# Layer weights by GpSimd's casting DMA, and q of every second pair turned by the DMA crossbar, in an attention-then-MLP kernel

## The chip, the cores and the metric

The kernel runs on one core of a Trainium2 chip. The metric is the device time of one execution in microseconds; lower is better. Times of one kernel are medians over its executions. A ratio is the mean time of one kernel's fast runs over the mean of the other's fast runs of the same rounds, so it is not quite the ratio of the medians quoted beside it. A result is called faster or slower only beyond 2%.

Names: PE is TensorE, PEld its weight loads, DVE VectorE, ACT ScalarE, POOL GpSimd, SP the sync engine, whose queue issues most DMAs. A transpose by the DMA crossbar is a DMA_TRANSPOSE in the trace, and a DMA's landing is its completion as the trace reports it. "L305" is a line of the kernel; the changed kernel's lines are shifted by up to 14 against those of the kernel before.

## The reference

```python
scores = q @ k.T / 8                      # 8 batches x 8 heads, 576 tokens, head size 64
thresh = max(scores, -1) - 0.02
scores = where(scores >= thresh, scores, -1e9)
attn   = softmax(scores)
x      = (attn @ v)                       # -> 4608 tokens x 512
h = x @ w_in;  g = h - tanh(h);  out = g @ w_out     # 512 -> 2048 -> 512, float32
```

## The kernel before

Two heads make a pair; there are 32 pairs (four to a batch), and each has nine tiles of 128 queries. Step s of the one big loop computes scores of tile s+7, makes shifted scores z of those of tile s+4, turns the z of tile s into softmax weights, and uses the weights of tile s-2 on v. From the second batch on, z is turned by a DMA through the crossbar (zT), and a share of the MLP of the batch before is put into every step. The kernel is emitted in a fixed order: each engine, and SP's queue, executes its instructions in that order.

q and k are split on GpSimd into two float16 halves (`hl`), turned on TensorE by nine transposes each, and copied out of PSUM by VectorE:

```python
def turn(p, t):
    hl = hls.pop((p, t))
    ps = ps_big.tile([P, W], FP16, name=f"ps_{t}", tag="big")
    for c in range(TPP):
        turn_chunk(ps[:, c * P : (c + 1) * P], c, hl[:, c, :, :].rearrange("p a d -> p (a d)"))
    m = qk_pool.tile([P, W], FP16, name=f"{t}T", tag=t)
    nc.vector.tensor_copy(out=m, in_=ps)
    mats[p, t] = m
    if t == "k":                          # kS: the halves swapped
        ...
            if p < HPAIR:
                nc.sync.dma_start(out=o, in_=i)
            else:
                nc.gpsimd.tensor_copy(out=o, in_=i)
```

The layer weights are loaded as float32 by SP into two buffers and cast by GpSimd; a load waits for the cast two before it:

```python
def w_cast():
    flat, wt, i, cols = loaded.pop(0)
    nc.gpsimd.tensor_copy(out=flat[:, i * cols : (i + 1) * cols], in_=wt)
def w_load(piece):
    ...
    wt = wt_pool.tile([P, cols], F32, name="wt", tag="wt")      # 2 buffers
    nc.sync.dma_start(out=wt, in_=s)
```

Preparation of a pair is planned by steps before its first score (LDK is 16), at the end of the step:

```python
PREP = ((LDK, load k), (LDK - 1, load q), (LDK - 2, load v), (8, split k), (7, split q),
        (5, turn k), (3, turn q), (4, split_v))
first = TPP * p - AHEAD                   # the step that holds the pair's first score
```

## Time and profile before

| | before |
|---|---|
| time, median of 4 | 557.35 us (556.17 to 559.22) |
| TensorE busy | 517.2 us of 555.2 us, 93% |
| TensorE busy from 250 to 300 us | 49.3 of 50 us |
| VectorE, ScalarE, GpSimd busy | 81%, 79%, 51% |
| DMA share from 250 to 300 us | 0.83 |

The table is read by stages. Until about 75 us attention of the first batch runs alone and TensorE has gaps; from 77 us the MLP is mixed in, and from about 140 us TensorE is nearly gapless; after 480 us only MLP is left. The lines are shown in the prediction.

### The profile page before, as it was taken

What the parts mean: (1) busy time and instruction counts of PE and PEld (TensorE: products, weight loads), DVE (VectorE), ACT (ScalarE), POOL (GpSimd) and SP (SyncE); (2) the same over time, 40 slices, a digit from 0 to 9 for tenths busy, and PEclk for the clock granted to TensorE, in tenths of its full rate; (3) what the DMA queues carried; (4) which work ended last, traced back from release to release, by engine and by line L of the source; (5) the groups of instructions that cost most, each with busy time, mean ns of one, the idle gap of its engine ahead of it and who ended that gap; (6) DMA issues with size and microseconds to landing.
All of it is one profiled execution on the core that took longest, in us unless ns stands there. A gap on an engine that the chain in (4) does not pass through costs nothing.

```text
span 555.2 us, 13146 instructions
## 1 busy us (share of the span) xinstructions
PE 517.2 (93%) x4806; PEld 296.8 (53%) x4806; DVE 450.5 (81%) x1210; ACT 439.5 (79%) x624; POOL 280.6 (51%) x378
## 2 busy tenths in 40 slices
PE   5787978889999999999999999999999999899997
PEld 2565645455555555555555555555555555444444
DVE  5877899998998999898988999888989998644440
ACT  4888879998988898889898898888988899733330
POOL 7466996666665565556556666656545650000000
PEclk9989999999999999999999999999999999999999
DMA  6776599887897798788888898889887775410103
GB/s 187 213 216 188 185 222 186 168 154 161 164 170 178 176 173 181 169 158 179 173 171 164 161 190 170 172 160 176 161 194 172 153 150 114 96 40 38 39 38 76
DMA packets 205280, 86.55 MB, mean 156 GB/s; under 512 B 172448, under 2 KB 197280, under 8 KB 205216
## 3 DMA queue, kind: packets, MB, share of 16 engines
q1 hardware_dynamic: 204624, 85.30, 71.1%
q8 instruction: 37, 0.61, 0.5%
q10 hardware_dynamic: 592, 0.43, 0.3%
q14 instruction: 27, 0.22, 0.1%
HBM read 37.75 MB, written 9.44 MB: 85 GB/s over the span
## 4 chain that ended last, share of the span: by engine, by line
PE 68%; DVE 14%; issue 6%; DMA 4%; POOL 4%; ACT 3%; SPq 1%; POOLq 0%; ACTq 0%; DVEq 0%
PE psY L483 20%; PE psH L457 16%; PE psS L292 15%; PE psO L402 5%; DVE sc L302 4%; DVE g L476 3%; PE psHt L457 2%; PE psS L282 2%; PE ps_q L217 2%; DMA zT<-z 2%; PE ps_k L217 2%; DVE nb L316 2%; DVE yo L493 2%; DVE qT L229 1%; PE psO L391 1%
## 5 line engine op out<-in xcount | busy, mean ns | idle before, releaser
L302 DVE TENSOR_SCALAR_CACHE_REDUCE sc<-psS 128x576 f32<-128x576 f32 x288 | 214.3, 751 | 17.2 <-PE psS L292 9.3
L336 ACT ACTIVATE z<-sc,nb 128x576 bf16<-128x576 f32 x256 | 192.4, 767 | 26.4 <-DVE nb L316 26.1
L373 ACT ACTIVATE pT<-zT 128x1152 f16<-128x1152 bf16 (+1 forms) x140 | 149.4, 1067 | 6.5 <-DMA zT<-z 4.8
L483 PE MATMUL psY<-w_out_sb,g 128*128 128x512 bf16 (+1 forms) x592 | 146.0, 374 | 0.0
L238 POOL COPY kS<-kT 64x1152 f16<-64x1152 f16 x56 | 63.9, 1141 | 142.3 <-DVE nb L316 141.0
L457 PE MATMUL psH<-xT,w_in_sb 128*128 128x512 bf16 x480 | 123.4, 379 | 2.3 <-DVE g L476 2.3
L292 PE MATMUL psS<-kT,qT 128*128 128x512 f16 (+1 forms) x512 | 106.2, 289 | 10.8 <-DVE nb L316 3.7
L292 PEld LDWEIGHTS <-qT 128*128 128x128 f16 x1024 | 77.1, 98 | 72.6 <-issue 17.7
L476 DVE SCALAR_TENSOR_TENSOR g<-th,psH 128x512 bf16<-128x512 f32 x128 | 87.2, 682 | 24.7 <-ACT th L470 24.7
L292 PE MATMUL psS<-kS,qT 128*128 128x512 f16 x496 | 102.3, 288 | 0.2 <-DMA kS<-kT 0.2
L470 ACT ACTIVATE th<-psH 128x512 f32<-128x512 f32 x128 | 74.8, 584 | 33.9 <-PE psH L457 33.3
L483 PEld LDWEIGHTS <-g 128*128 128x128 bf16 x592 | 50.9, 98 | 56.5 <-issue 3.1
L457 PEld LDWEIGHTS <-w_in_sb 128*128 128x128 bf16 x576 | 48.9, 98 | 59.1 <-issue 5.6
L402 PEld LDWEIGHTS <-pT 128*128 128x128 f16 x1280 | 55.9, 98 | 26.0 <-ACT pT L373 3.0
L402 PE MATMUL psO<-vb,pT 128*128 128x65 bf16 x1280 | 61.6, 194 | 0.6 <-ACT pT L373 0.6
L316 DVE TENSOR_SCALAR nb<-mx 128x2 f32<-128x2 f32 (+1 forms) x160 | 42.9, 268 | 0.8
L179 POOL TENSOR_TENSOR qhl<-xs,qhl 128x576 f16<-128x576 f32 x31 | 39.7, 1279 | 2.7
L179 POOL TENSOR_TENSOR khl<-xs,khl 128x576 f16<-128x576 f32 x31 | 39.6, 1279 | 2.6
L217 PE MATMUL ps_k<-ident_f,khl 128*128 128x128 f16 x288 | 22.2, 223 | 13.9 <-POOL khl L179 7.4
L229 DVE COPY qT<-ps_q 128x1152 f16<-128x1152 f16 x31 | 23.5, 757 | 11.0 <-PE ps_q L217 10.9
L365 ACT ACTIVATE pT<-psZ 128x640 f16<-128x640 bf16 (+1 forms) x36 | 23.6, 655 | 10.4 <-PE psZ L356 10.3
L493 DVE COPY yo<-psY 128x512 f32<-128x512 f32 (+1 forms) x31 | 21.1, 680 | 10.7 <-PE psY L483 6.7
(71 smaller groups left out, 522.2 us busy)
## 6 DMA issues: line engine op xcount, KB each, us to landing
vraw<-in_v_dram SPq DMA_DIRECT2D x32, 256.0 KB, 3.5
out_dram<-yo SPq DMA_DIRECT2D x32, 256.0 KB, 2.8
kraw<-in_k_dram SPq DMA_DIRECT2D x31, 256.0 KB, 3.2
qraw<-in_q_dram SPq DMA_DIRECT2D x31, 256.0 KB, 3.7
wt<-in_moe_w_in_dram SPq DMA_DIRECT2D x8, 512.0 KB, 4.8
wt<-in_moe_w_out_dram SPq DMA_DIRECT2D x8, 512.0 KB, 4.3
vraw<-in_v_dram SPq DMA_DIRECT2D x64, 32.0 KB, 3.0
zT<-z SPq DMA_TRANSPOSE x112, 3.4
```

The source lines that it names most:

```text
L179: nc.gpsimd.tensor_tensor(out=hl[:, :, 1, :], in0=x, in1=hl[:, :, 0, :], op=ALU.subtract)
L238: nc.gpsimd.tensor_copy(out=o, in_=i)
L292: nc.tensor.matmul(out=ps[:, dst], lhsT=lhs, rhs=kk[:, src], start=(n == 0), stop=(n == 1),)
L302: nc.vector.tensor_scalar(out=sc, in0=ps[:, lo : lo + S], scalar1=SC, scalar2=None, op0=ALU.mult, op1=ALU.max, accum_out=mx[:, c : c + 1],)
L316: nc.vector.tensor_scalar(out=nb[:, 0:n], in0=mx[:, 0:n], scalar1=-1.0, scalar2=tau, op0=ALU.mult, op1=ALU.add,)
L336: nc.scalar.activation(out=z, in_=sc, func=ACT.Prelu, bias=nb, scale=1.0, alpha=STEEP)
L373: nc.scalar.activation(out=pt[:, 0 : n * P], in_=zts.pop(i)[:, 0:n, :], func=ACT.Exp)
L402: nc.tensor.matmul(out=po[:, (j - 1 - 5 * hh) + ab, :], lhsT=pt[:, blk * P : (blk + 1) * P], rhs=vb[:, hh, c, :], start=(n == 0), stop=(n ...
L457: nc.tensor.matmul(out=ps, lhsT=w_in_sb[:, c, n * P : (n + 1) * P], rhs=xs[m][:, c, :] if m < B else xR[:, c, :, :], start=(c == 0), stop= ...
L470: nc.scalar.activation(out=th, in_=ps, func=ACT.Tanh)
L476: nc.vector.scalar_tensor_tensor(out=gs[m][:, n, :], in0=th, scalar=-1.0, in1=ps, op0=ALU.mult, op1=ALU.add,)
L483: nc.tensor.matmul(out=ps, lhsT=gs[m][:, n, ms * P : (ms + 1) * P], rhs=w_out_sb[:, n, cols], start=(n == 0), stop=(n == DF_C - 1),)
```

## The change

The intent: let GpSimd's queue load and cast the weights in one DMA, so that no cast and no wait for a buffer is left; and take nine transposes and a copy of every second q from TensorE and VectorE.

```diff
-    wt_pool = pool("wt", 2)
...
+    def q_by_dma(p):
+        return p >= 2 * HPAIR and p % 2 == 1
+
     def turn(p, t):
         hl = hls.pop((p, t))
+        if t == "q" and q_by_dma(p):
+            m = mats[p, t] = qk_pool.tile([P, W], FP16, name=f"{t}T", tag=t)
+            nc.sync.dma_start_transpose(
+                out=m.rearrange("p (c r) -> p c r", c=TPP),
+                in_=hl.rearrange("p c a d -> p (c a d)"),
+            )
+            return
...
         if j == 4:
+            qrem = REM
+            if q_by_dma(p):
+                qrem = (slice(512, 640, 2), slice(513, 640, 2))
-                            lhsT=qT[:, REM[hh]], rhs=kk[:, srcs[hh]],
+                            lhsT=qT[:, qrem[hh]], rhs=kk[:, srcs[hh]],
...
-            if s + AHEAD in w_when:
-                if loaded:
-                    w_cast()
-                piece = next(pieces, None)
-                if piece:
-                    w_load(piece)
+        if s + AHEAD in w_when:
+            dst, src = next(pieces)
+            nc.gpsimd.dma_start(out=dst, in_=src)
```

## The prediction

> **What bounds the kernel now.** I read the page first, then the busy time by stage, then the chain of waits for the first 140 us, and last the timelines of single engines around one pair boundary.
>
> ```profile
> PE 517.2 (93%) x4806; PEld 296.8 (53%) x4806; DVE 450.5 (81%) x1210; ACT 439.5 (79%) x624; POOL 280.6 (51%) x378
> ...
> DMA  6776599887897798788888898889887775410103
> ```
>
> ```profile
> 28.00:50.00 22.00, 19.77 (x271) 14.51 (x271) 18.36 (x57) 19.24 (x32) 13.71 (x19) 0.94 0.68 188
> 50.00:75.00 25.00, 18.89 (x238) 13.39 (x238) 19.56 (x54) 18.75 (x31) 22.69 (x28) 0.93 0.74 214
> ...
> 250.00:300.00 50.00, 49.29 (x469) 28.04 (x467) 45.47 (x124) 44.40 (x61) 31.35 (x43) 1.00 0.83 173
> ```
>
> The columns are window, length, busy us of PE, PEld, DVE, ACT, POOL, then clock, DMA share, GB/s. There are two regimes. From about 140 us PE is busy for 49.3 of 50 us and sets the pace; DVE and ACT stand at 91% and 89%. Before 75 us PE has gaps, and POOL is at 22.7 of 25. The POOL timeline says why:
>
> ```profile
> 22.90 1.04 POOL L584 CAST w_in_sb<-wt 128x1024 bf16<-128x1024 f32 x1 [6.16 <-DMA wt<-in_moe_w_in_dram]
> ...
> 36.48 1.04 POOL L584 CAST w_in_sb<-wt 128x1024 bf16<-128x1024 f32 x1 [3.87 <-DMA wt<-in_moe_w_in_dram]
> ...
> 51.12 1.04 POOL L584 CAST w_in_sb<-wt 128x1024 bf16<-128x1024 f32 x1 [4.92 <-DMA wt<-in_moe_w_in_dram]
> ```
>
> POOL stands still in front of a cast whose load has not landed. The splits of the next pair's k and q queue behind it, so TensorE turns k late, and ScalarE waits in turn (4.42 us at 57.57 us). The chain of waits from 15.7 to 54.9 us lies wholly on POOL. So the weights are on the path early, and TensorE is the path later.
>
> **What the skill says.** (1) The Trainium skill, "DMA: Bandwidth & Descriptors", section "SWDGE vs HWDGE vs iDMA": a cast in a DMA needs the GpSimd queue, a plain DMA transpose the SP or ACT queue. The change obeys both; the trace shows all 140 transposes on SP. (2) The same page, "Issuing engines are not separate DMA queues": all issuers share 16 DMA engines, and another issuer saves only issuing time. So the weights' 8 MB still pass through these engines; what goes is the buffer and the wait. No run here shows GpSimd's issuing cost yet. (3) The same page, "Anatomy of one DMA": a fixed cost near 2.0 us, mostly the receipt. The trace agrees: a full transpose lands about 1.97 us (median of two of the groups) after its 1.3 us issue ends, also when another went just ahead.
>
> **Part A, weights.** It removes 16 casts (16 x 1.04 = 16.6 us of POOL), POOL's 15.7 us wait for the loads, and 16 loads from the SP queue. It adds 16 issues on POOL, perhaps 1 us each (my guess), none with a wait. What it is worth is read from ScalarE: from its first pT (18.3 us) to the end of its last of the first batch (71.6 us) 53.3 us pass, of which it idles 9.1 us (2.01, 0.17, 0.45, 1.03, 0.22, 4.42, 0.25, 0.28, 0.23). Where it is unhindered, one tile takes 1.21 to 1.25 us (z and pT, e.g. five tiles from 33.36 to 39.39); 36 tiles need 44 to 45 us. That would gain 8 to 9 us. TensorE, at 90% and a clock of 0.94, and the later k loads will keep some; less weight traffic at 75 to 100 us, where DMA is at 0.99 and one zT takes 6.56 us, gives some. I book -7 us.
>
> **Part B, q of 12 pairs (9, 11, ... 31).** Removed per pair: nine transposes on TensorE and one DVE copy.
>
> ```profile
> L229 DVE COPY qT<-ps_q 128x1152 f16<-128x1152 f16 x31 | 23.5, 757 | 11.0 <-PE ps_q L217 10.9
> ...
> zT<-z SPq DMA_TRANSPOSE x112, 3.4
> ```
>
> The chain gives ps_q x9 as 0.52 us of TensorE, so 12 x 0.52 = 6.2 us of the bound; the copies are 12 x 0.76 = 9.1 us of DVE, which is beside the path. Added: 12 transposes of the same shape as the full zT (128 x 1152, two bytes), 12 x 1.32 = 16 us of SP issuing and 12 x 1152 = 13,800 packets, 7% of 205,280. If nothing waited, B would be -6 us.
>
> But q must be there when the next pair's first score is due, and the issue keeps its place in the program: end of the step three before it, in order on SP, behind that step's zT. Here is the boundary to pair 13, first SP, then PE:
>
> ```profile
> 181.97 1.25 SPq L344 DMA_TRANSPOSE zT<-z  x1
> ...
> 187.74 0.57 SPq L139 DMA_DIRECT2D vraw<-in_v_dram  x1
> 188.37 0.66 SPq L145 DMA_DIRECT2D vraw<-in_v_dram  x1
> 189.08 0.62 SPq L146 DMA_DIRECT2D vraw<-in_v_dram  x1
> 189.80 1.32 SPq L344 DMA_TRANSPOSE zT<-z  x1
> 191.22 1.24 SPq L344 DMA_TRANSPOSE zT<-zm  x1
> ```
>
> ```profile
> 190.00 0.67 PE L217 MATMUL ps_q<-ident_f,qhl 128*128 128x128 f16 x9
> ...
> 192.38 0.41 PE L292 MATMUL psS<-kT,qT 128*128 128x512 f16 x2
> ```
>
> SP is solidly occupied from 181.97 to 192.46: seven raw loads lie in it. The zT whose z was ready at 187.52 is issued at 189.80, 2.3 us late, by SP's own queue. The new q transpose goes in at 191.2, lands 3.25 us later (the median of full transposes back to back) at 194.5, and pair 13's first score, at 192.38 on PE now, waits until then. PE works in order, so all its later work waits too. Now q needs only 0.5 us on PE and 0.76 us on DVE from there.
>
> The same reading for all twelve: landing (end of that zT issue + 0.1 + 3.25) less the present start of the first score gives, for pairs 9, 11, ... 31: 4.5, 2.7, 2.1, 2.4, 3.2, 2.7, 2.6, 2.0, 2.9, 4.3, 2.2 and -0.6 us (pair 31 has no loads left in front of it). Sum of the positive ones: 31.6 us. The 0.5 us that PE saves is already inside, since the landing, not PE, sets the start.
>
> Part of it comes back. In odd pairs that follow a batch's first pair (9, 13, ... 29) the MLP work has run out at the boundary, steps last about 1 us and DVE is about 1 us behind PE; DVE has no q copy any more and empties its queue during the stall: 6 x about 1 us. Elsewhere TensorE idles only 1.4%, so some 0.2 us per pair. I take 31.6 - 6 - 2.5 = 23, with some doubt about whether SP gains lead in the stall, so +20 us. Can it? ScalarE leads as far as its inputs let it: it waits for nb just after each boundary (0.80 us at 191.7) and for psH before it (1.07 us at 188.59). The zT at 181.97 followed its z by 0.03 us. A stall at one odd boundary therefore gives no lead at the next odd one, two pairs later.
>
> Sum: 557.6 - 7 + 20 = about 571 us.
>
> **Rivals.** (a) *q lands in time.* Then -7 - 6 = 544 us, 2.4% faster. For it: POOL has q split some 9 us before (182.1 for pair 13), the lateness is only SP's, and pair 31 shows that without loads SP is prompt; and somebody chose "every second pair", which smells of trying. Against it: nothing in the diff moves the issue earlier. (b) *DMA becomes the bound.* It stands at 0.83 in the steady stage and transposes are most of the packets; 7% more on average puts the changed pairs near 0.9. Landings grow (zT's longest is 6.6 us now) and ScalarE's pT begins to wait: a further 5 to 10 us, about 578. Against it: ScalarE waits only 4.8 us for zT in the whole run. (c) *Part A gains nothing.* GpSimd's descriptor making or round-robin with the first zT transposes at 65 to 75 us eats it: 577. Against it: POOL has 15.7 us of plain waiting to give. (d) *Strided weights.* The changed pairs read the middle tile's q with a step of two; 8 loads of 109 ns in each, which lie beside matmuls; were they twice as long, 12 x 0.9 = 10 us at most, likely far less.
>
> **Range and chances.** A lies between -9 and -2, B between -6 (rival a) and +30; the two ends together are unlikely, so 548 to 584. The 2% lines are 546.4 and 568.7. The centre lies just above the upper one: 0.54 slower, 0.36 within, 0.10 faster.
>
> **What would show it.** In the changed trace: no POOL wait for weights before 75 us, and the first zT (now 67.91 us) some 6 us sooner; ps_q x180 and 19 copies on DVE; twelve SP transposes qT<-qhl between a zT and the zT<-zm; TensorE waits on "DMA qT<-qhl" in front of L292, about eleven of 2 to 4 us, and TensorE's share in the steady stage falling from 98.5% to about 93%. The prediction is wrong if these waits are under 0.5 us each (rival a), if ScalarE's wait for zT rises above 10 us (b), or if the first batch ends as late as now (c).

## The result, and the profile after

| | before | after |
|---|---|---|
| time, median of 4 | 557.35 us | 598.78 us (597.35 to 604.43) |
| ratio | | 1.0759 (95%: 1.0683 to 1.0835), slower |
| mean granted clock | 0.994 | 0.967 |

The direction was forecast, the size was not: 598.8 us lies outside the range of 548 to 584 us. First the page of the changed kernel: busy time, then the clock and DMA in 40 slices.

```profile
PE 515.2 (86%) x4631; PEld 294.3 (49%) x4698; DVE 446.5 (75%) x1198; ACT 443.2 (74%) x624; POOL 274.4 (46%) x378
...
PEclk9899999997989899998989899998989899999999
DMA  5867697788787978688567969799677976500003
```

TensorE is busy for almost as long as before in a span that is 41 us longer, and its clock, which was 9 in every slice but one before, dips to 7 or 8 again and again. The stages, with the columns as in the prediction:

```profile
28.00:50.00 22.00, 17.39 (x252) 12.76 (x250) 18.38 (x52) 18.16 (x31) 14.18 (x20) 1.00 0.69 132
50.00:75.00 25.00, 22.86 (x333) 16.66 (x331) 23.71 (x77) 24.46 (x39) 16.36 (x23) 1.00 0.73 151
...
250.00:300.00 50.00, 45.31 (x416) 25.87 (x420) 42.26 (x117) 41.73 (x57) 28.18 (x38) 0.97 0.74 162
```

From 50 to 75 us TensorE does more than before (22.9 us against 18.9), from 28 to 50 us less (17.4 against 19.8), and in the steady stage it falls from 49.3 to 45.3 of 50 us. The list of waits says what for (total us, number, longest):

```profile
PE psS L305 <- DMA qT<-qhl: 38.7, 11, 5.7
...
PE psS L305 <- DMA kS<-kT: 7.2, 2, 4.6
```

The boundary to pair 13, which the prediction took as its example, SP first and then PE:

```profile
199.82 1.31 SPq L357 DMA_TRANSPOSE zT<-z  x1
201.24 1.50 SPq L228 DMA_TRANSPOSE qT<-qhl  x1
202.84 1.23 SPq L357 DMA_TRANSPOSE zT<-zm  x1
```

```profile
204.88 0.42 PE L305 MATMUL psS<-kT,qT 128*128 128x512 f16 x2 [3.74 <-DMA qT<-qhl]
205.13 0.43 PE L305 MATMUL psS<-kS,qT 128*128 128x512 f16 x2
205.38 0.67 PE L305 MATMUL psS<-kT,qT 128*128 128x512 f16 x2
```

The q transpose goes out behind the zT, as read from the old trace, and TensorE waits 3.74 us. The third line holds what the prediction had not seen: half a microsecond after the wait the same two matmuls take 0.67 us where they took 0.42. The trace's clock records show half clock from 205.38 us for 3.41 us. There are nine such records between 120 us and the end of the run, 34.1 us in all, and every one begins during one of the eleven waits or within 1.4 us after it; in the kernel before there were two, both before 60 us (each trace has one more as its last matmuls end).

To place the loss, I took from both traces the time of each pair's first score, and the lengthening of the interval from one pair's to the next:

| intervals | forecast for the odd ones | measured |
|---|---|---|
| to pairs 1 to 8, together (no q part yet) | | +0.4 us |
| to the odd pairs 9, 11, ... 31 | 4.5 2.7 2.1 2.4 3.2 2.7 2.6 2.0 2.9 4.3 2.2 -0.6 | 4.7 2.9 2.8 1.7 2.7 3.1 2.9 1.7 3.8 2.4 2.3 -0.5: +30.6 us |
| to the even pairs 10, 12, ... 30 | small gains | +9.6 us |

0.4 + 30.6 + 9.6 = 40.6 us of the 40.8 us between the two profiled spans (41.4 us between the medians). The even intervals that follow pairs 15 and 23, the two shortest waits (2.0 and 2.1 us), where no half clock was recorded, are longer by 0.0 us; of the others, all are longer by 0.9 to 1.7 us but the first, to pair 10, in a stretch where TensorE had idle time to spare before the change (17.0 of 20 us busy from 120 to 140 us).

### The profile page after: what moved, and what is told of

It reads as the page before. It is cut to its first block, busy times and chain, and to the rows that moved or that the text cites. A ratio compares the mean times of both kernels' runs of the same rounds, so it can differ in the third digit from the quotient of the medians.

```text
span 596.0 us, 12843 instructions
## 1 busy us (share of the span) xinstructions
PE 515.2 (86%) x4631; PEld 294.3 (49%) x4698; DVE 446.5 (75%) x1198; ACT 443.2 (74%) x624; POOL 274.4 (46%) x378
## 4 chain that ended last, share of the span: by engine, by line
PE 58%; DVE 17%; DMA 12%; POOL 5%; issue 5%; ACT 2%; SPq 0%; POOLq 0%; DVEq 0%; ACTq 0%
PE psY L496 16%; PE psS L305 14%; PE psH L470 14%; DMA qT<-qhl 6%; DVE sc L315 5%; PE psO L415 4%; DVE g L489 4%; PE psS L295 3%; DMA kS<-kT 2%; PE psHt L470 2%; POOL kS L248 2%; DVE kT L239 2%; DVE yo L506 2%; DVE nb L329 1%; PE ps_q L216 1%
## 5 line engine op out<-in xcount | busy, mean ns | idle before, releaser
L305 PE MATMUL psS<-kT,qT 128*128 128x512 f16 (+1 forms) x512 | 109.8, 298 | 47.1 <-DMA qT<-qhl 38.7
L496 PE MATMUL psY<-w_out_sb,g 128*128 128x512 bf16 (+1 forms) x556 | 141.8, 378 | 2.5 <-issue 0.8
L305 PEld LDWEIGHTS <-qT 128*128 128x128 f16 x1024 | 76.5, 101 | 117.4 <-DMA qT<-qhl 40.0
L470 PE MATMUL psH<-xT,w_in_sb 128*128 128x512 bf16 x451 | 120.9, 385 | 3.8 <-DVE g L489 1.9
L305 PE MATMUL psS<-kS,qT 128*128 128x512 f16 x496 | 105.4, 295 | 7.2 <-DMA kS<-kT 7.2
L415 PEld LDWEIGHTS <-pT 128*128 128x128 f16 x1280 | 57.5, 100 | 28.0 <-ACT pT L386 4.1
L415 PE MATMUL psO<-vb,pT 128*128 128x65 bf16 x1280 | 63.2, 196 | 1.8 <-ACT pT L386 1.8
L329 DVE TENSOR_SCALAR nb<-mx 128x2 f32<-128x2 f32 (+1 forms) x160 | 45.4, 284 | 0.8
L430 DVE TENSOR_TENSOR osb<-psO,rc 128x256 bf16<-128x256 f32 x64 | 27.2, 424 | 2.2
```

What stands on the lines that cost most here:

```text
L305: nc.tensor.matmul(out=ps[:, dst], lhsT=lhs, rhs=kk[:, src], start=(n == 0), stop=(n == 1),)
L329: nc.vector.tensor_scalar(out=nb[:, 0:n], in0=mx[:, 0:n], scalar1=-1.0, scalar2=tau, op0=ALU.mult, op1=ALU.add,)
L415: nc.tensor.matmul(out=po[:, (j - 1 - 5 * hh) + ab, :], lhsT=pt[:, blk * P : (blk + 1) * P], rhs=vb[:, hh, c, :], start=(n == 0), stop=(n ...
L470: nc.tensor.matmul(out=ps, lhsT=w_in_sb[:, c, n * P : (n + 1) * P], rhs=xs[m][:, c, :] if m < B else xR[:, c, :, :], start=(c == 0), stop= ...
L496: nc.tensor.matmul(out=ps, lhsT=gs[m][:, n, ms * P : (ms + 1) * P], rhs=w_out_sb[:, n, cols], start=(n == 0), stop=(n == DF_C - 1),)
```

## The experiments

All were correct and ran in rounds of three beside the kernel before (medians 557.2 to 558.1 us); each time is a median of four. One execution of the third run below, of 566.0 us, counted as slow and is not in its ratio. Intervals, waits and clock records are those of the one profiled execution of each version.

**1. The weights' part alone** (`e1_weights_only`).

```diff
     def q_by_dma(p):
-        return p >= 2 * HPAIR and p % 2 == 1
+        return False
```

> The weights' part alone: q of all pairs on TensorE again. Theory (the part is worth nothing because the three weight loads that GpSimd now issues at 13.9 to 16.9 us hold up the copy of kS, and v, and what is won later is lost again at the sixth pair): within 3 us of before, about 557 to 558 us; TensorE waits some 7 us for the kS copy before 40 us; the first score of pair 8 within 1 us of before's 117.04 us. Rival 1 (the part is worth what I forecast, and the q part costs the difference): about 550 us. Rival 2 (the weights' part costs time itself, through GpSimd's issues): 565 us or more.

Measured: 552.78 us, ratio 0.9936 (0.9871 to 1.0001), executions 551.51, 551.51, 554.05 and 559.21 us. Neither my theory (nothing) nor the forecast (-7 us) is confirmed: the part is worth some 3 to 6 us in three executions, and the fourth is 1.8 us slower than the median before. Its early stage varies although its instructions up to pair 8 are the same as the change's: the profiled execution reached pair 8's first score 4.8 us sooner than before, that of the change 0.4 us later.

**2. The q part alone** (`e2_q_only`): the kernel before with only the hunks of `turn` and of the middle tile.

> The q part alone: weights loaded and cast as before. Theory (all of the loss lies here): 595 to 600 us, eleven TensorE waits for q's landing of 38 us in all, and some 8 to 10 records of half clock after 120 us. Rival 1 (each part takes half): about 578 us. Rival 2 (the q part as forecast, 20 us, and an interaction of the parts for the rest): about 577 us too, but with the first score of pair 9 later by less than 2 us.

Measured: 599.47 us, ratio 1.0771 (1.0717 to 1.0826); waits for q 38.7 us in 11; odd intervals +30.6 us, even ones +10.4 us. The whole loss is the q part.

**3. q issued three steps sooner** (`e3_q_early`), the rest as in the change.

```diff
         for d, f in PREP[3 if p == 1 else 0 :]:
+            if d == 3 and q_by_dma(p):
+                d = 6
             plan.setdefault(first - d, []).append(lambda p=p, f=f: f(p))
```

> The whole change, but the transpose of q for the 12 pairs is issued three steps sooner, ahead of the raw loads on SP. Theory (only the place in SP's order makes the crossbar's q late): no TensorE wait for q above 0.3 us, no half clock after 60 us, and the 6 us of transposes saved: 549 to 553 us. Rival (the 7% more DMA traffic is itself too much, or the strided weights of the middle tile are slow): 560 us or more, with ScalarE waiting more than 10 us for zT, or weight loads of the middle tile well above 109 ns.

Measured: 560.87 us, ratio 1.0028 (0.9973 to 1.0084). The waits for q are gone (0.3 us in all), which takes back the loss; but the promised gain is not there. The list of waits shows the new one:

```profile
ACT pT L386 <- DMA zT<-z: 21.2, 24, 2.3
```

Before, it read:

```profile
ACT pT L373 <- DMA zT<-z: 4.8, 6, 1.5
```

The time and the waits are those that the rival gave, and two half-clock records came after 60 us where the theory had none. Of the rival's two reasons, the strided weights are out: middle-tile weight loads, which step by two in the 12 pairs, took 110 ns at the median in the change (106 to 115), 109 before. Its other reason, more DMA traffic, is not told apart from SP's order by this run. The q transpose now stands in front of the raw loads on SP, and everything behind it is later: in the even pairs the zT of tiles 1 and 3 were issued 3.6 and 4.3 us after their z, against 1.9 and 3.0 us before. The intervals show where the gain went: the odd ones are 8.2 us shorter than before, the even ones 12.3 us longer.

**4. TensorE kept busy during the wait** (`e6_keep_busy`), the rest as in the change; the products go nowhere, the result is unchanged.

```diff
+        if j == 0 and q_by_dma(p):
+            pw = ps_o.tile([P, 6, D + 1], F32, name="psW", tag="o")
+            for _ in range(14):
+                nc.tensor.matmul(out=pw.rearrange("p a d -> p (a d)"), lhsT=ident_bf,
+                                 rhs=w_in_sb[:, 0, 0 : 6 * (D + 1)], start=True, stop=True)
         qT, kT, kS = mats[p, "q"], mats[p, "k"], mats[p, "ks"]
```

> The whole change, with 14 useless matmuls of 128x390 (about 2.3 us together) put on TensorE just where it waits for q, into a free accumulator. Theory (after a long wait the clock is granted at half for 3.41 us, and that is what makes the loss 10 us larger than the waits): the waits shrink by the matmuls' time, the half-clock records after 120 us go from nine to three or fewer, and the time falls by 8 to 15 us, to 584 to 591 us, though TensorE does more. Rival (the extra loss in the even pairs comes from late zT or from DMA, not from the clock): same as the change, 597 to 601 us, or longer by the matmuls that don't fit in the wait.

Measured: 592.47 us, ratio 1.0628 (1.0564 to 1.0691), no half clock after 120 us. It fell by 6.3 us against the change, a little short of the 8 to 15 us expected, and its early stage happened to be 6.2 us late in the profiled execution. So it was repeated without the weights' part.

**5. The same without the weights' part** (`e9_q_keep_busy`): edit 4 on experiment 2.

> The q part alone with the 14 useless matmuls in front of each late first score, to repeat the test of the clock without the varying early stage. Theory: no half clock after 120 us, waits for q in all smaller by about the matmuls' time, 585 to 591 us against 599.5 us of the q part alone. Rival: 597 us or more.

Measured: 590.82 us, ratio 1.0591 (1.0537 to 1.0645), against 599.47 us: 8.7 us less with 168 more matmuls. One half-clock record is left after 120 us, at pair 9. The even intervals went from +10.4 to -3.1 us, while the odd ones grew from 30.6 to 37.4 us: where the wait was short or absent (pair 31: 2.8 us) the useless work itself is paid. The clock of experiment 2, then of this one, in 40 slices:

```profile
PEclk9988999997989899998989899998989899999999
```

```profile
PEclk9998999998999999999999999999999999999999
```

That the clock makes the even pairs longer is shown.

**6. Weights by GpSimd, kS of the first pairs copied by GpSimd** (`e4_w_ks_pool`): experiment 1 and

```diff
-                if p < HPAIR:
+                if False:
                     nc.sync.dma_start(out=o, in_=i)
```

> The weights' part alone, with the copy of kS of the first pairs made by GpSimd, as for all later pairs, instead of by a DMA. In the profiles so far the same instructions reach the first score of pair 8 at 117.4 (the change), 112.3 (weights alone), 116.1 and 123.2 us (two further versions), against 117.0 before: the early stage of the new weights varies. Theory (the kS copies by DMA share the engines with weight loads that nothing holds back any more, and how long they take is chance): no wait for a kS DMA, the spread of the executions under 4 us, median 549 to 552 us. Rival (the v loads, or DMA as a whole, are what varies): spread of 6 us or more as in the weights alone (551.5 to 559.2), median 552 to 557 us.

Measured: 550.58 us, ratio 0.9872 (0.9827 to 0.9918), executions 550.04 to 551.52 us. The spread shrank from 7.7 to 1.5 us and the median is 6.6 us under before. In the change, GpSimd issues three weight loads by 16.9 us, and no buffer holds them back; TensorE stood before kS, whose copies SP had issued at 16.0 to 17.2 us (PE timeline of the change):

```profile
24.24 0.46 PE L305 MATMUL psS<-kS,qT 128*128 128x512 f16 x2 [4.58 <-DMA kS<-kT]
```

In the kernels with the old weights those copies landed in 2.3 to 4.0 us (median 2.5 us in the kernel before), in the four with the new weights in 2.3 to 7.6 us. In those four the first score of pair 8 came at 112.3, 116.1, 117.4 and 123.2 us, after TensorE waits for kS of 2.7, 7.4, 7.2 and 9.9 us; in the five versions with GpSimd's copies (this one and experiments 9 to 12) at 109.8 to 112.8 us. That the kS copies by DMA make the early stage late and variable is shown; the spread of whole times has other sources too (7.3 us in experiment 12); and how much of the 6.6 us this version owes to GpSimd's copies as such, without the new weights, was not run.

**7. Raw loads five steps later, q part alone** (`e5_q_loads_later`), q at its place in the change.

```diff
+            if d >= LDK - 2 and p > 2 * HPAIR:
+                d -= 5
             plan.setdefault(first - d, []).append(lambda p=p, f=f: f(p))
```

> The q part alone, q issued at its place in the change, but the raw loads of k, q and v five steps later from pair 9 on, so that SP has them behind the q transpose and not in front of it. Theory (the q transpose is late because seven raw loads keep SP busy in front of it): the zT ahead of it follows its z at once, q lands some 4.8 us after that z, waits for q fall from 38 us to under 8 us in all, no half clock after 120 us: 550 to 558 us. Rival (the transpose itself is too slow, or DMA is full): waits stay above 20 us, 580 us or more.

Measured: 559.50 us, ratio 1.0022 (0.9964 to 1.0080), waits for q 9.8 us. The waits fell from 38.7 us by three quarters, a little less than expected, and the time by 40 us. The zT before q followed its z by 0.2 us on average. One half-clock record came after 120 us, where none was expected. So the raw loads in front of it on SP made q late. The time is 1.5 us above what I expected: the loads now delay the zT behind them (tile 8 in even pairs: 2.75 us after its z), and ScalarE waits 16.0 us for zT.

**8. Raw loads issued by GpSimd, q part alone** (`e7_q_loads_gpsimd`).

```diff
-        eng = nc.sync
+        eng = nc.gpsimd if p > 2 * HPAIR else nc.sync
```

> The q part alone, at its place in the change, with the raw loads from pair 9 on issued by GpSimd instead of SP. Theory (SP's order): as with the later loads, waits for q under 8 us in all and no half clock after 120 us, 550 to 558 us; GpSimd pays 7 x 0.6 us a pair, which it has. Rival (the loads' traffic, not their issue, makes the transposes late): the same traffic still stands in front, waits above 20 us, 580 us or more.

Measured: 566.49 us, ratio 1.0151 (1.0095 to 1.0207; unclear at 2%), waits for q 13.8 us in 6, and three half-clock records after 120 us. It lies between the two forecasts. SP's lag is gone (zT 0.03 us after their z, the zm 0.1 to 0.25 us), but four of the twelve q now land 4.7 to 5.5 us after issue where 3.3 to 3.9 us was usual in the change. Both theories have a part: most of the lateness was SP's order, and by these landings the loads' traffic beside the transposes costs the rest.

**9. Loads dealt out to SP's free places** (`e10_slots`): experiment 6 with the q part and

```diff
+            if p > 2 * HPAIR:
+                d = {LDK: 12, LDK - 1: 12, LDK - 2: 11}.get(d, d)
+            if d == 3 and q_by_dma(p):
+                d = 5
```

> A version meant to beat both: weights by GpSimd with the kS copies of the first pairs made by GpSimd (550.6 us by itself), q of the 12 pairs by the crossbar two steps sooner, behind the zT of tile 1, and from pair 9 on the raw loads dealt out to where SP has room (k and q behind the zT of tile 3, v behind the zm). Theory (SP's in-order queue is what made q late, and what made ScalarE wait for zT when q came early in front of the loads): waits for q under 3 us in all, ScalarE's waits for zT under 8 us, no half clock after 120 us, 544 to 547 us, the 6 us of transposes won at last. Rival (DMA traffic: 12 more transposes lengthen the landings whatever the order): 550 us or more with ScalarE's waits for zT above 12 us.

Measured: 551.27 us, ratio 0.9888 (0.9856 to 0.9920). Waits for q: 0.3 us. By its time and by ScalarE's waits (below) the rival came; whether for the rival's reason, the control shows.

**10. The control** (`e11_slots_no_q`): the same with `q_by_dma` false.

> The control: the same loads in the same places, q of all pairs on TensorE. Theory: nothing waits for the loads either way, so 549 to 552 us as with the weights and kS alone, and the difference to the version with q by the crossbar is the transposes' 0.5 us a pair, 6 us. Rival (the load order itself is worth something): below 548 us.

Measured: 551.60 us, ratio 0.9888 (0.9857 to 0.9919). Equal to experiment 9: the 6 us do not show in the whole times. The steady stage of the control, then that of experiment 9 (columns as above):

```profile
250.00:350.00 100.00, 96.88 (x919) 56.11 (x933) 90.38 (x245) 87.13 (x122) 55.93 (x72) 1.00 0.83 170
```

```profile
250.00:350.00 100.00, 96.66 (x900) 55.07 (x915) 89.58 (x244) 88.53 (x123) 59.15 (x77) 1.00 0.94 184
```

DMA goes from 0.83 to 0.94, and from 140 to 470 us ScalarE waits 17.6 us for zT and 5.2 us for the zm, against 2.1 us for zT in the control:

```profile
ACT pT L386 <- DMA zT<-z: 2.1, 4, 0.9
```

```profile
ACT pT L386 <- DMA zT<-z: 17.6, 17, 2.3
```

TensorE has less to do in each pair, but its share stays the same (96.7% against 96.9%). The intervals tell more than the whole times: against the kernel before, the odd ones of experiment 9 are 9.4 us shorter and the even ones 6.8 us longer; in the control the sums are -0.1 and +0.3 us. So from pair 8 to 31 experiment 9 is 2.9 us quicker than the control; before pair 8, where both issue the same instructions, it happened to be 1.6 us later. Most of what the odd boundaries win is lost again at the even ones. From pair 9 on a full zT goes out 1.28 us after its z on average, 0.58 us in the control, and lands in 3.66 us, 3.54 us in the control: by these averages, of one execution each, it is SP's queue more than the fuller DMA engines that holds the zT back in this order.

**11. q of all 24 pairs from the third batch** (`e12_slots_all_q`): `q_by_dma` true for p >= 8.

> The same with q of all 24 pairs from the third batch by the crossbar. Theory (as long as SP has room for one more transpose in each pair, each is worth 0.5 us of TensorE): 539 to 543 us. Rival (SP and DMA are full: SP then has 12.7 us of issues in a pair of 14.3 us, DMA about 0.9): no better than with every second pair, or worse, with ScalarE's waits for zT above 15 us.

Measured: 550.02 us, ratio 0.9853 (0.9814 to 0.9893). TensorE's share from 250 to 350 us falls to 94.1%, DMA stands at 0.99 there, and ScalarE waits 32.5 us for zT and zm. From pair 8 to 31 it is no quicker than before (+0.6 us). Twice as many transposes moved, and no gain beyond the spread (548.35 to 551.94 us).

**12. q early and the raw loads by GpSimd** (`e13_gpsimd_early`): experiment 6 with the q part at d = 5 and the edit of experiment 8.

> Weights and kS copies by GpSimd as in the 550.6 us version, q of the 12 pairs by the crossbar behind the zT of tile 1, and the raw loads from pair 9 on issued by GpSimd at their old steps, so that SP holds transposes and stores alone. It tells apart why q by the crossbar saved nothing (551.3 us against 551.6 us) when no wait for q was left. If SP's occupation holds the zT back: every zT follows its z within 0.3 us, ScalarE's waits for zT fall from 23 us in the steady stage to under 6 us, 544 to 547 us. If the DMA engines themselves are full (0.88 to 0.94 in the steady stage): the zT issue at once but land in 4 us or more instead of 3.4, ScalarE waits as long, 550 us or more.

Measured: 550.81 us, ratio 0.9890 (0.9842 to 0.9938), executions 547.59, 550.51, 551.11 and 554.86 us. In the profiled execution, the fastest, nearly every zT follows its z at once (0.03 to 0.6 us) and ScalarE's waits in the steady stage fall to 4.0 us, as the first theory expects; but the zT of tiles 1 and 3 land in 4.6 to 5.0 us on average (4.1 and 3.6 before) and q in 5.7 us, as the second does, and TensorE waits for q twice, 1.0 and 2.0 us. That execution wins 2.9 us between pairs 8 and 31, as that of experiment 9 wins 2.7; the other executions do not show it in their time. So SP's order (experiment 9) and longer landings (here, with the raw loads on GpSimd) each hold the transposes back; why half of the 6 us stays lost when ScalarE hardly waits is open.

Versions 6 and 9 to 12 are about 8% faster than the change, and faster than the kernel before by a margin clear of noise, yet under 2%. Version 6 is the simplest, and only experiment 9 spreads less (1.2 us against 1.5); q by the crossbar adds nothing to it that the whole times show.

## Why the prediction was wrong

The forecast was 557.6 - 7 + 20 = 570.6 us; 598.8 us came. By its own steps:

- **"Sum of the positive ones: 31.6 us" was right.** The odd intervals grew by 30.6 us, pair by pair within 0.9 us of the list but for pair 27 (4.3 forecast, 2.4 measured). That q goes out behind the zT, that seven raw loads on SP make it late, and that a stall gives no lead at the next odd boundary, held; experiments 3 and 7 show the cause.
- **"Part of it comes back", 6 x about 1 us and 0.2 us per pair, failed.** Instead of giving back 8.5 us, the even intervals cost 9.6 us more. I had taken a stall as lost time only. It also lowers the granted clock: each stall that left TensorE idle for most of a clock window was followed by 3.41 us at half clock. Experiment 5 removes the stalls' idleness, not the stalls, and the even intervals turn from +10.4 to -3.1 us: the recovery that I forecast exists, a third of the size I gave it, once the clock stays up: 0.6 us at five of the six places named (pairs 14, 18, ... 30) and nothing elsewhere. That VectorE's catching up makes it was not traced. This is 18 us of the miss. The trace of the kernel before had the sign: half clock from 27.3 and 54.6 us, behind stalls, of which I used the mean clock of 0.94 alone. The Trainium skill, "TensorE: Matmul & The Clock Gate", section "Part 1: The HAM clock gate", says that TensorE falls to half rate after an idle window of about 3.4 us, free-running; I had computed stalls of 2 to 4.5 us and did not consult it. The trace agrees in length and rate (records of 3.41 us, or 6.83, at 0.5), not in how idle the window must be (see the end).
- **"I book -7 us" for the weights failed in this kernel.** In the change they brought +0.4 us by pair 8 in the profiled execution, and 0.7 us less between the medians of the q part alone and of the change. GpSimd's waits for the weights did go, and TensorE ran better from 50 to 75 us. But the wait had also kept the weight traffic down to two buffers; without it the kS copies of the first pairs land late (7.2 us of TensorE's waits), and so does v (GpSimd waits 12.1 us for it, 2.3 before). Rival (c) named this end and its sign came, with other transfers as the victim: the first batch ends at 70.6 us against 71.6. With kS copied by GpSimd it ends at 62.5 us, the 8 to 9 us of the forecast, and the median falls by 6.6 us; that this is close to 7 is in part luck, since the change of the copies is in it. This is 7 us of the miss.
- **The last 3 us** are the step from 23 to 20, taken "with some doubt" in the wrong direction. 18 + 7 + 3 - 1 (30.6 against 31.6) makes 27 of the 28 us.
- **Rival (a), "q lands in time" making 544 us, was wrong too.** In experiments 3 and 9 q did land in time, and the whole times show nothing of the 6 us of TensorE's transposes; between pairs 8 and 31 the profiled execution of experiment 9 has half of them. I had said against rival (b) that ScalarE waits only 4.8 us for zT; from 140 to 470 us its waits for zT and zm went from 3.3 us to 22.9 us in experiment 9, by SP's order more than by full DMA engines. The strided weights, rival (d), cost nothing.
- **The signs.** ps_q x180, 19 copies and twelve transposes between a zT and the zm came as forecast; the first zT, "some 6 us sooner", came at 67.6 us against 67.9. "About eleven of 2 to 4 us": eleven, of 2.0 to 5.7 us. TensorE's steady share, forecast at 93%, was 88% (245.9 of 280 us from 200 to 480 us).

## What to carry to other kernels

Before moving a transfer into an in-order queue, write down when the consumer needs it, what stands in front of it in that queue, and add the landing time: that gave each stall to within about a microsecond (off by 1.9 us for pair 27). Count a TensorE stall that fills most of 3.4 us as more than its length, because the clock dropped after nine of the eleven here. And when a wait is removed, ask what it was holding back: the two weight buffers kept the DMA engines free for kS, and TensorE's own transposes of q kept SP's queue, and the DMA engines, free for zT.

## What the Trainium skill lacked or had wrong

- "TensorE: Matmul & The Clock Gate", Part 1, says that half clock comes after an idle window. The windows need not be wholly idle here: laying the 3.41 us grid of the clock records over TensorE's busy time of the change and of experiment 2 (from 100 us on), every full-clock window with 2.06 us of idle or more was followed by half clock, and none with 1.73 us or less was (in experiments 3 and 5, windows with 1.90 and 1.96 us were too). The section on a second failure mode of the same page speaks of short idles between groups of matmuls; the page gives no such share.
- "DMA: Bandwidth & Descriptors", section "Latency and other measured facts", gives about 1 us to the first byte of a DMA issued by GpSimd, as the Q7's emission; it has no figure for the time that GpSimd's own queue is held. Here the issue of a weight piece with its cast took 0.53 to 0.80 us of it, against 1.04 us for the cast that it replaced.
